# Moving the first 128 rows of w_down from the end of the load queue to its middle, as sixteen loads

## The chip, the cores and the metric

The kernel runs on one core of one Trainium2 chip. The metric is the device time of one execution in microseconds, as the median of several runs. A core has five engines with instruction streams of their own: TensorE (PE; its weight loads are listed as PEld), VectorE (DVE), ScalarE (ACT), GpSimd (POOL) and SyncE (SP). Here SP issues all but one of the loads from the chip's memory (HBM). A load is carried out by 16 DMA engines, each of which counts the load's semaphore up by one when its share has landed; whoever needs the data waits for the full count of 16.

## The reference

One token is decoded through an attention block and a gated MLP, with layer norms ahead and residual sums behind:

```python
scores = einsum("bhqd,bhkd->bhqk", q, k) * (Dh ** -0.5)   # q = layernorm(x) @ wq
p = softmax(scores);  o = einsum("bhqk,bhkd->bhqd", p, v)
h = x + o.reshape(B, Sq, Hq * Dh) @ wo
g = layernorm(h) @ w_gate;  u = layernorm(h) @ w_up
out = h + (gelu(g) * u) @ w_down
```

There are 32 heads of width 128, a cache of 4096 positions, a model width D of 640, and a hidden width DF of 1728. All inputs are bf16. K and V take 33.6 MB each; w_down, with 1728 x 640 elements, takes 2.2 MB.

## The kernel before

The heads are worked off in eight groups of four (`NG`, `HG`). For each group SP loads 4 MB of K and 4 MB of V. There are two buffers for each (`kbuf`, `vbuf`), so that the load of K for group n+2 waits until the last multiplication of group n has read its buffer (`kfree[n]`), and a V load until the products with V of two groups before are done (`vfree`). For each group DVE multiplies K by the query (L339), TensorE sums over the head width with an identity matrix (L348), DVE reduces (L355), ACT forms the exponentials (L384), and TensorE multiplies by V (L395). The work of neighbouring groups is interleaved by hand in the loop over n (from L453), and at the loop's end SP issues the next V and K loads; for n = 3 these are V of the fourth group and K of the sixth.

All order is written out by hand. The class `Sched` collects a list of instructions per engine with the semaphores that each waits for. What SP issues runs through one queue in the order of issue: wq, K 0, K 1, V 0, then K and V by turns, wo in two parts with the last V load between them, w_gate, w_up, and then w_down. The weights of the MLP lie over the K and V buffers (`over`), so w_gate, w_up and w_down wait for the last readers of these.

w_down is loaded in two ways. Its last 64 rows come in eight loads of four partitions (L581), which follow w_up in the queue. Its first 1664 rows are 13 column blocks of 128 rows; `WD_PARTS` groups these in loads of 5, 4, 3 and 1 blocks (L586). In a load of n blocks, partition p holds the n successive rows n*p to n*p+n-1 of the part; `WD_COLS` gives the columns of w_gate and w_up that belong to block s, so that the hidden values come out in the same order.

The tail runs like this. `up` multiplies the normed h by w_gate (into pg) and by w_up (into pu), 70 matmuls each (L648). DVE and ACT form gelu(g)*u, ending in `hm` (L664). Then for each of the 13 blocks and the two remainders four matmuls (L686) add to the output in PSUM. Their order is: five blocks; the small product `rest` (L670), which spreads the remainder's hidden values; four blocks; the two remainders; four blocks. Each waits for its own load. Then DVE copies the sum (L690), and SP writes it out (L691).

Of the kernel before, what the change touches and what calls it, by code (L numbers as in the profile page):

```python
# [6 lines left out]
BF16 = mybir.dt.bfloat16  # L7
# [4 lines left out]
D = 640  # L12
# [20 lines left out]
DJ = 128 // HW  # L33
NFT = 13
NF = NFT + 1
WD_PARTS = (5, 4, 3, 1)

WD_COLS = []
for _n in WD_PARTS:
    _b = 128 * len(WD_COLS)  # L40
# [73 lines left out]
def bass_sequential_preLN__gqa_block_cached__glu_gated_geglu__decode_kernel(  # L114
# [12 lines left out]
    S = Sched(nc)  # L127

    def sb(name, shape, dt):
        return nc.alloc_sbuf_tensor(name, shape, dt)  # L130
# [7 lines left out]
    def over(name, base, shape):  # L138
        return nc.alloc_sbuf_tensor_at(name, shape, BF16, offset=nc.lookup_mloc(base).addr)
# [3 lines left out]
    wg_sb = over("wg_sb", kbuf[NG % 2], [128, NC_D, DF])  # L143
    wu_sb = over("wu_sb", kbuf[(NG + 1) % 2], [128, NC_D, DF])
    wd_sb = over("wd_sb", vbuf[NG % 2], [128, NFT + NRR, D])

    NPR = 3
    prod = [sb("prod%d" % i, [128, RP, DH], BF16) for i in range(NPR)]
# [8 lines left out]
    xm = sb("xm", [VM, VR, DH], FP32)  # L157
# [7 lines left out]
    csel = sb("csel", [128, HW], BF16)  # L165
    jred = sb("jred", [128, DJ], FP32)
    cred = sb("cred", [128, HW], FP32)
    x_sb = sb("x_sb", [1, D], BF16)
    x32 = sb("x32", [128, NC_D], FP32)
    h32 = sb("h32", [128, NC_D], FP32)  # L170
    sq = sb("sq", [128, NC_D], FP32)
# [12 lines left out]
    hm = sb("hm", [128, NF], BF16)  # L184
# [65 lines left out]
    def cache(src, g):  # L250
        return src[0, g * HG:(g + 1) * HG, :, :].rearrange("h (q r) d -> (h q) r d", r=R)
# [4 lines left out]
    def load_k(g):  # L256
        d_k[g] = S.dma("sync", "k%d" % (g % 2), lambda s: s.dma_start(
            kbuf[g % 2][:, :, :], cache(A_k_cache, g)), [kfree[g - 2] if g >= 2 else None])


    def load_v(g):
        d_v[g] = []
        cuts = [0, R]
        for i in range(len(cuts) - 1):
            lo, hi = cuts[i], cuts[i + 1]
            tok = S.dma("sync", "v%d_%d" % (g % 2, i), lambda s, lo=lo, hi=hi: s.dma_start(
                vbuf[g % 2][:, lo:hi, :], cache(A_v_cache, g)[:, lo:hi, :]),
                [vfree[g - 2] if g >= 2 else None])
            d_v[g] += [tok] * (hi - lo)
# [44 lines left out]
    def query(g):  # L314
        tok = None
        for c in range(NC_D):
            n0 = g * HG * DH
            tok = S.op("tensor", lambda t, c=c, n0=n0: t.matmul(  # L318
                pq[:, :], xb[:, c, :], wq_sb[:, c, n0:n0 + HG * DH],
                start=(c == 0), stop=(c == NC_D - 1)),  # L320
                [t_xb, d_wq, t_qb[g - 1] if g else None], token=(c == NC_D - 1))
        for hh in range(HG):
            lo, hi = hh * PPH, (hh + 1) * PPH
            t_qb[g] = S.op("scalar", lambda a, lo=lo, hi=hi, hh=hh: a.copy(  # L324
                qb[lo:hi, g, :], pq[lo:hi, hh * DH:(hh + 1) * DH]), [tok])
        return tok
# [10 lines left out]
    def mult(g, s):  # L337
        n = g * NP + s
        return S.op("vector", lambda v: v.tensor_tensor(  # L339
            out=prod[n % NPR][:, :, :], in0=kbuf[g % 2][:, s * RP:(s + 1) * RP, :],  # L340
            in1=qb[:, g, :].unsqueeze(1).to_broadcast([128, RP, DH]), op=ALU.mult),
            [d_k[g], t_qb[g], fold_done.get(n - NPR)])

    def fold(g, s, t_mult):
        n = g * NP + s
        W = 512 // RP
        for j in range(DH // W):
            fold_done[n] = S.op("tensor", lambda t, j=j: t.matmul(  # L348
                pf[n % 2][:, :], Ibf[:, :], prod[n % NPR][:, :, j * W:(j + 1) * W],
                start=(j == 0), stop=(j == DH // W - 1)),  # L350
                [t_mult, t_ibf, red_done.get(n - 2)], token=(j == DH // W - 1))

    def red(g, s):
        n = g * NP + s
        red_done[n] = S.op("vector", lambda v: v.reduce_sum(  # L355
            sc[g % 2][:, s * RP:(s + 1) * RP],
            pf[n % 2][:, :].rearrange("p (r w) -> p r w", r=RP), axis=AX.X),
            [fold_done[n], t_exp[g - 2] if g >= 2 else None])
# [3 lines left out]
    def top(g):  # L362
        t_mx[g] = S.op("vector", lambda v: v.reduce_max(  # L363
            mx[:, g:g + 1], sc[g % 2][:, :], axis=AX.X), [red_done[g * NP + NP - 1]])

    def turn(g):
        t_mm[g] = S.op("tensor", lambda t: t.matmul(  # L367
            pm[0:1, 0:128], mx[:, g:g + 1], I32[:, :], start=True, stop=True),
            [t_mx[g], t_i32, t_exp[g - 1] if g else None])

    def head(g):
        t_mr[g] = S.op("vector", lambda v: v.reduce_max(  # L372
            mrow[0:1, g * HG:(g + 1) * HG],
            pm[0:1, 0:128].rearrange("p (h q) -> p h q", h=HG), axis=AX.X), [t_mm[g]])
# [46 lines left out]
    def total(w):  # L421
        t_zz[0] = S.op("tensor", lambda t: t.matmul(
            pz[:, 0:HW], ones[:, :], RS[:, w * HW:(w + 1) * HW], start=True, stop=True),
            [t_exp[2 * w + 1], t_aP[w - 1] if w else None])
# [14 lines left out]
    def place(w, b):  # L439
        t_aP[w] = S.op("vector", lambda v: v.tensor_copy(  # L440
            aP[:, w * HW:(w + 1) * HW], pz[:, 16:16 + HW]), [b])
# [4 lines left out]

    CH = NV // 4

    query(0)
    query(1)  # L450
    t_mul = {}
    t_g = None
    for n in range(NG - 1):  # L453
        w = (n - 3) // 2 if n >= 3 and n % 2 else None
        p, o = n - 1, n - 2
        beside = p >= 0 and n < NG - 2

        t_mul[0] = mult(n, 0)
        if p >= 0:
            red(p, NP - 1)  # L460
            top(p)
        if w is None and n >= 4:
            place((n - 4) // 2, t_g)
        t_mul[1] = mult(n, 1)

        fold(n, 0, t_mul[0])
        if p >= 0:
            turn(p)
            head(p)
        if o >= 0:  # L470
            values(o, 3 * CH, NV)
        fold(n, 1, t_mul[1])
        red(n, 0)
        t_mul[2] = mult(n, 2)
        if p >= 0:
            soft(p)
        if w is not None:
            total(w)
        if 2 <= n + 1 < NG:
            t_qlast = query(n + 1)  # L480
        fold(n, 2, t_mul[2])
        red(n, 1)
        if w is not None:
            invert(w)
        if o >= 0:
            extract(o)
        t_mul[3] = kfree[n] = mult(n, 3)
        if o >= 0:
            column(o)
        if beside:  # L490
            values(p, 0, CH)
        fold(n, 3, t_mul[3])
        red(n, 2)
        if w is not None:
            spread(w, [(po[:, w * HW:(w + 1) * HW], 0, HW, t_acc[o])])
        if beside:
            values(p, CH, 2 * CH)
        if w is not None:
            t_g = gather(w)
        if beside:  # L500
            values(p, 2 * CH, 3 * CH)

        if n == 0:
            load_k(2)
            load_v(1)
        elif n == NG - 3:
            load_k(n + 2)
            load_v(n)
        else:
            if n >= 2:  # L510
                load_v(n)
            if n + 2 < NG:
                load_k(n + 2)
# [65 lines left out]
    for h in range(2):  # L579
        for j in range(4):  # L580
            d_wdr = S.dma("sync", "wdr", lambda s, h=h, j=j: s.dma_start(  # L581
                wd_sb[32 * h + j:32 * h + NRP:4, NFT:NFT + NRR, :], rows[h, j]), [t_zr])
    d_wd = []
    for i, n in enumerate(WD_PARTS):
        s0 = len(d_wd)
        tok = S.dma("sync", "wd%d" % i, lambda s, s0=s0, n=n: s.dma_start(  # L586
            wd_sb[:, s0:s0 + n, :],
            B_w_down[128 * s0:128 * (s0 + n), :].rearrange("(p i) n -> p i n", i=n)), [vfree[NG - 2]])
        d_wd += [tok] * n
# [34 lines left out]
    NQ = D // 4  # L624
# [39 lines left out]
    t_hm = S.op("vector", lambda v: v.tensor_mul(hm[:, :], gu[:, :], pu[:, 0:NF * WIDE:WIDE]), [a, t_u])  # L664
# [9 lines left out]
    def down(s, j):  # L674
        if s >= NFT:
            return hr[0:NRK, s - NFT:s - NFT + 1], wd_sb[0:NRK, s, j * NQ:(j + 1) * NQ]
        return hm[:, s:s + 1], wd_sb[:, s, j * NQ:(j + 1) * NQ]

    n = sum(WD_PARTS[0:2])
    order = list(range(n)) + list(range(NFT, NFT + NRR)) + list(range(n, NFT))  # L680
    for i, s in enumerate(order):
        if s == WD_PARTS[0]:
            t_hr = rest()
        for j in range(4):
            last = i == len(order) - 1
            b = S.op("tensor", lambda t, s=s, j=j, last=last: t.matmul(  # L686
                pd[32 * j:32 * j + 1, 0:NQ], *down(s, j),
                start=False, stop=last, skip_group_check=True),
                [t_hr if s >= NFT else t_hm, d_wd[s]], token=(last and j == 3))
    t_o = S.op("vector", lambda v: v.tensor_copy(o_sb[:, :], pd[:, 0:NQ]), [b])  # L690
    d_o = S.dma("sync", "out", lambda s: s.dma_start(  # L691
        out[0, 0, :].rearrange("(j i) -> j i", j=4), o_sb[0:128:32, :]), [t_o])
# [32 lines left out]
```

## Time and profile before

| what | value |
|---|---|
| median of 3 runs | 203.91 us (203.9 to 204.17) |
| profiled execution: span from first to last instruction | 202.33 us |
| median less that span | 1.58 us |
| TensorE busy | 155.4 us, 77% of the span |
| VectorE busy | 116.4 us, 58% |
| ScalarE busy | 30.7 us, 15% |
| moved from HBM | 84.23 MB, 416 GB/s over the span |
| mean granted TensorE clock | 0.930 |

The page gives no other time for the profiled execution than its span, so sums are made against the span, and the 1.58 us between span and median stands for what lies around it. A line of the profile names an engine, a line of the kernel (L686), an operation, and output and input by name; "<-DMA wd_sb..." in brackets says what ended the idle time before it. PEld rows are weight loads of TensorE, which run ahead of the matmuls. "SPq" rows are issues of loads on SP. The DMA share of a stretch is the busy time of packets that start in it, over 16 engines. Below the views, the trace records each DMA packet with its start, duration and size, and each count of a load's semaphore; it does not record which of the 16 engines carried a packet.

### The profile page before, as it was taken

How to read it: one execution, taken by the hardware profiler on the slowest of the kernel's cores; microseconds unless marked ns; L12 is line 12 of the kernel's file. 1: busy time of each engine (PE TensorE's matmuls, PEld its weight loads, DVE VectorE, ACT ScalarE, POOL GpSimd, SP SyncE). 2: the span in 40 equal slices, each digit the busy share in tenths (PEclk: the TensorE clock that was granted, in tenths of full speed). 3: DMA queues.
4: the chain of work that ended last, by engine and by line, in shares of the span. 5: the costliest groups of instructions: out<-in, count | busy, mean ns of one | idle time of the engine just before them, and what ended most of it. 6: DMA issues, size and time to landing. Idle time of an engine off the chain costs nothing.

```text
span 202.3 us, 2515 instructions
## 1 busy us (share of the span) xinstructions
PE 155.4 (77%) x1084; PEld 71.0 (35%) x1084; DVE 116.4 (58%) x153; ACT 30.7 (15%) x110; POOL 2.4 (1%) x8
## 2 busy tenths in 40 slices
PE   1005349689959997996899499979777999978675
PEld 1001013233323432432343134324323344667562
DVE  6200087998097919953993488569999513301121
ACT  2002200007000600420060004200604004000000
POOL 1000000000000000000000000000000000200000
PEclk9999999999979999999999979999999999985555
DMA  7999999999999999999999999999999899999993
GB/s 259 437 437 415 421 441 473 428 415 415 418 453 460 421 416 415 424 449 447 428 428 415 424 447 447 421 434 415 428 444 441 380 429 461 441 383 437 434 388 117
DMA packets 3940, 84.38 MB, mean 417 GB/s; under 512 B 441, under 2 KB 570, under 8 KB 986
## 3 DMA queue, kind: packets, MB, share of 16 engines
q1 hardware_dynamic: 3928, 84.23, 97.4%
q8 instruction: 8, 0.13, 0.3%
q14 instruction: 2, 0.02, 0.0%
q10 hardware_dynamic: 2, 0.00, 0.0%
HBM read 84.23 MB, written 0.00 MB: 416 GB/s over the span
## 4 chain that ended last, share of the span: by engine, by line
DMA 59%; DVE 24%; PE 15%; issue 1%; SPq 0%; DVEq 0%
DMA kbuf<-in_A_k_cache_dram 46%; DVE prod L339 16%; DMA wu_sb<-in_B_w_up_dram 13%; PE pf L348 8%; PE pu L395 4%; DVE sc L355 3%; DVE xz L413 2%; PE pu L648 1%; DVE xm L410 1%; PE pf L686 1%; PE pg L395 1%; DVE mx L363 0%; DVE mrow L372 0%; PE pm L367 0%; SPq L247 0%
## 5 line engine op out<-in xcount | busy, mean ns | idle before, releaser
L339 DVE TENSOR_TENSOR prod<-kbuf,qb 128x4096 bf16<-128x4096 bf16 x32 | 72.8, 2278 | 45.0 <-DMA kbuf<-in_A_k_cache_dram 45.0
L348 PE MATMUL pf<-prod,Ibf 128*128 128x512 bf16 x256 | 66.5, 408 | 23.0 <-DVE prod L339 22.9
L348 PEld LDWEIGHTS pf<-prod,Ibf 128*128 128x128 bf16 x256 | 24.4, 103 | 62.3 <-DVE prod L339 29.5
L395 PE MATMUL pg<-vbuf,P 128*16 128x512 bf16 x128 | 29.9, 379 | 0.0
L355 DVE TENSOR_REDUCE sc<-pf 128x32 f32<-128x512 f32 x32 | 21.6, 676 | 4.8 <-PE pf L348 4.7
L395 PE MATMUL pu<-vbuf,P 128*16 128x512 bf16 x96 | 22.2, 379 | 0.0
L318 PE MATMUL pq<-wq_sb,xb 128*128 128x512 bf16 x40 | 12.1, 441 | 12.3 <-DMA wq_sb<-in_A_wq_dram 11.1
L380 ACT ACTIVATE nb<-pm 128x4 f32<-128x4 f32 x8 | 1.4, 175 | 118.5 <-PE pm L377 118.5
L384 ACT ACTIVATE P<-sc,nb 32x128 bf16<-32x128 f32 x32 | 18.6, 580 | 0.9
L395 PEld LDWEIGHTS pg<-vbuf,P 128*16 128x16 bf16 x128 | 10.6, 89 | 14.5 <-issue 1.3
L395 PEld LDWEIGHTS pu<-vbuf,P 128*16 128x16 bf16 x96 | 8.1, 90 | 11.7 <-issue 1.7
L324 ACT CAST qb<-pq 32x128 bf16<-32x128 f32 x32 | 8.2, 258 | 15.8 <-PE pq L318 15.0
L318 PEld LDWEIGHTS pq<-wq_sb,xb 128*128 128x128 bf16 x40 | 3.8, 110 | 17.1 <-issue 12.8
L384 ACT ACTIVATION_READ_ACCUMULATOR P<-sc,nb 32x1 f32 x32 | 8.0, 251 | 0.0
L601 PE MATMUL pf<-aP,wo_sb 128*128 128x32 bf16 x160 | 7.1, 194 | 0.8 <-issue 0.6
L413 DVE TENSOR_REDUCE xz<-xm 16x128 f32<-16x512 f32 x7 | 7.3, 1044 | 0.2
L601 PEld LDWEIGHTS pf<-aP,wo_sb 128*128 128x128 bf16 x160 | 6.8, 131 | 1.5 <-issue 1.1
L403 PE MATMUL pq<-P,vbuf 128*128 128x32 bf16 x128 | 3.6, 188 | 1.4 <-DMA vbuf<-in_A_v_cache_dram 1.4
L410 DVE TENSOR_TENSOR xm<-pg,rmask 16x512 f32<-16x512 f32 x4 | 2.7, 670 | 3.4 <-PE pg L395 3.4
L293 ACT ACTIVATE ln<-pz,ln 128x1 f32<-128x1 f32 x2 | 0.5, 263 | 23.9 <-DVE ln L290 23.9
L403 PEld LDWEIGHTS pq<-P,vbuf 128*128 128x128 bf16 x128 | 3.5, 104 | 1.5 <-DMA vbuf<-in_A_v_cache_dram 1.5
L410 DVE TENSOR_TENSOR xm<-pu,rmask 16x512 f32<-16x512 f32 x3 | 1.9, 643 | 3.2 <-PE pu L395 3.2
(84 smaller groups left out, 56.4 us busy)
## 6 DMA issues: line engine op xcount, KB each, us to landing
kbuf<-in_A_k_cache_dram SPq DMA_DIRECT2D x8, 4096.0 KB, 25.2
vbuf<-in_A_v_cache_dram SPq DMA_DIRECT2D x8, 4096.0 KB, 22.8
wq_sb<-in_A_wq_dram SPq DMA_DIRECT2D x1, 5120.0 KB, 15.1
wo_sb<-in_A_wo_dram SPq DMA_DIRECT2D x1, 3840.0 KB, 28.7
wg_sb<-in_B_w_gate_dram SPq DMA_DIRECT2D x1, 2160.0 KB, 22.5
wu_sb<-in_B_w_up_dram SPq DMA_DIRECT2D x1, 2160.0 KB, 27.1
wo_sb<-in_A_wo_dram SPq DMA_DIRECT2D x1, 1280.0 KB, 17.8
wd_sb<-in_B_w_down_dram SPq DMA_DIRECT2D x1, 800.0 KB, 15.8
```

The costliest lines, as they stand in the source:

```text
L318: tok = S.op("tensor", lambda t, c=c, n0=n0: t.matmul(pq[:, :], xb[:, c, :], wq_sb[:, c, n0:n0 + HG * DH], start=(c == 0), stop=(c == NC_D ...
L324: t_qb[g] = S.op("scalar", lambda a, lo=lo, hi=hi, hh=hh: a.copy(qb[lo:hi, g, :], pq[lo:hi, hh * DH:(hh + 1) * DH]), [tok])
L339: return S.op("vector", lambda v: v.tensor_tensor(out=prod[n % NPR][:, :, :], in0=kbuf[g % 2][:, s * RP:(s + 1) * RP, :], in1=qb[:, g, :]. ...
L348: fold_done[n] = S.op("tensor", lambda t, j=j: t.matmul(pf[n % 2][:, :], Ibf[:, :], prod[n % NPR][:, :, j * W:(j + 1) * W], start=(j == 0) ...
L355: red_done[n] = S.op("vector", lambda v: v.reduce_sum(sc[g % 2][:, s * RP:(s + 1) * RP], pf[n % 2][:, :].rearrange("p (r w) -> p r w", r=R ...
L384: t_exp[g] = S.op("scalar", lambda a, lo=lo, hi=hi, h=h, hh=hh: a.activation(P4[g % 2][lo:hi, :, hh], sc[g % 2][lo:hi, :], ACTF.Exp, bias= ...
L395: t_pv[g] = S.op("tensor", lambda t, i=i, r=r, last=last: t.matmul(pv[g % 2][0:VM, :], P4[g % 2][:, r:r + VR, :], vbuf[g % 2][:, r:r + VR, :],
L403: t_pv[g] = S.op("tensor", lambda t, r=r: t.matmul(pq[:, 0:WIDE], vbuf[g % 2][:, r, :], P4[g % 2][:, r, :].unsqueeze(1).to_broadcast([128, ...
L410: a = S.op("vector", lambda v: v.tensor_tensor(out=xm[:, :, :], in0=pv[g % 2][0:VM, :].rearrange("p (r d) -> p r d", r=VR), in1=rmask[:, : ...
L413: t_ext[g] = S.op("vector", lambda v: v.reduce_sum(xz[g % 2][:, :], xm[:, :, :].rearrange("p r d -> p d r"), axis=AX.X), [a, t_acc[g - 2] ...
L601: tok = S.op("tensor", lambda t, c=c, cc=cc, first=first, last=last: t.matmul(pp[:, cc * WIDE:(cc + 1) * WIDE], wo_sb[:, w, c, cc::NC_D], ...
L648: b = S.op("tensor", lambda t, s=s, c=c, part=part, first=first, last=last: t.matmul(ps[:, s * WIDE:(s + 1) * WIDE], part, hln[:, c:c + 1] ...
```

## The change

The first 128 rows of w_down get a tile of their own, `wd_pre`, and are loaded by sixteen loads of 15, 14, ..., 1 and 8 rows, issued by SP in the loop at n = 3, right after K of the sixth group. They have two semaphores, eight loads on each. The parts of w_down in the tail become 1, 5, 4, 2 and 1 blocks, of which the first is the moved one and is skipped there; the matmuls read block 0 from `wd_pre`, the small product comes after five blocks as before, and the remainders come after ten blocks instead of nine. To make room, `x_sb` lies over `xm`, which is written much later.

```diff
-WD_PARTS = (5, 4, 3, 1)
+WD_PARTS = (1, 5, 4, 2, 1)
+PRE = (15, 14, 13, 12, 11, 10, 9, 8, 7, 6, 5, 4, 3, 2, 1, 8)
...
+    wd_pre = sb("wd_pre", [128, D], BF16)
...
-    x_sb = sb("x_sb", [1, D], BF16)
+    x_sb = over("x_sb", xm, [1, D])
...
-        if n == 0:
+        if n == 3:
+            load_v(n)
+            load_k(n + 2)
+            p0 = 0
+            for m in PRE:
+                d_wpre = S.dma("sync", "wpre%d" % (len(d_pre) // 8), lambda s, p0=p0, m=m: s.dma_start(
+                    wd_pre[p0:p0 + m, :], B_w_down[p0:p0 + m, :]))
+                d_pre.append(d_wpre)
+                p0 += m
+        elif n == 0:
...
-    d_wd = []
+    d_wd = [d_pre[-1]]
     for i, n in enumerate(WD_PARTS):
+        if i == 0:
+            continue
         s0 = len(d_wd)
...
+        if s == 0:
+            return hm[:, 0:1], wd_pre[:, j * NQ:(j + 1) * NQ]
         return hm[:, s:s + 1], wd_sb[:, s, j * NQ:(j + 1) * NQ]
 
-    n = sum(WD_PARTS[0:2])
+    n = sum(WD_PARTS[0:3])
     order = list(range(n)) + list(range(NFT, NFT + NRR)) + list(range(n, NFT))
     for i, s in enumerate(order):
-        if s == WD_PARTS[0]:
+        if i == 5:
             t_hr = rest()
...
-                [t_hr if s >= NFT else t_hm, d_wd[s]], token=(last and j == 3))
+                [t_hr if s >= NFT else t_hm, d_wd[s], d_pre[7]], token=(last and j == 3))
```

More of the change, by code (lines that the diff above doesn't have):

```diff
@@ L447, in bass_sequential_preLN__gqa_block_cached__glu_gated_geglu__decode_kernel @@
     CH = NV // 4
+    d_pre = []
     query(0)
```

## The prediction

> **What bounds the kernel now.** I read the page first, for the share of each engine and of the DMA queues; then the chain of waits in its last 40 us; then the timeline of the weight loads and of SP's queue; then stretches of time for the DMA share; and last the trace's single DMA records: the 16 completion counts that every load sends, one from each DMA engine, and the times and sizes of packets. From the page:
>
> ```profile
> DMA  7999999999999999999999999999999899999993
> ...
> q1 hardware_dynamic: 3928, 84.23, 97.4%
> q8 instruction: 8, 0.13, 0.3%
> ```
>
> The one queue with all of SP's loads keeps the 16 DMA engines busy for 97.4% of the span. What comes later in it lands later, unless it lies in a gap. The second line counts eight fetches of instructions on the same engines; they matter below. From the chain of waits (start, us, what):
>
> ```profile
> 167.66 27.13 DMA wu_sb<-in_B_w_up_dram
> 194.79 0.05 issue
> 194.84 2.54 PE pu L648 x70
> 197.38 0.03 issue
> 197.41 0.02 DVEq L106
> 197.43 0.04 issue
> 197.47 0.18 DVE hm L664
> 197.65 0.04 issue
> 197.69 0.84 PE pf L686 x20
> ```
>
> The end hangs on the landing of w_up at 194.79; 2.90 us later the matmuls with w_down begin. The timeline of TensorE's weight loads shows a second tie:
>
> ```profile
> 198.57 0.36 PEld L686 LDWEIGHTS pf<-wd_sb,hm 128*1 128x1 bf16 x16
> 199.20 0.10 PEld L686 LDWEIGHTS pf<-wd_sb,hr 48*1 48x1 bf16 x8 [0.27 <-issue]
> 199.57 0.23 PEld L686 LDWEIGHTS pf<-wd_sb,hm 128*1 128x1 bf16 x12 [0.26 <-DMA wd_sb<-in_B_w_down_dram]
> 199.94 0.09 PEld L686 LDWEIGHTS pf<-wd_sb,hm 128*1 128x1 bf16 x4 [0.15 <-DMA wd_sb<-in_B_w_down_dram]
> ```
>
> The last two groups also wait for w_down, whose last load lands at 199.90. So two limits end within about 0.1 us of each other: TensorE's own pace after w_up, and the end of the queue. A gain needs both to come earlier; a loss needs only one of them later.
>
> The completion counts show that the 16 engines (I call them lanes) are not level. Those of w_up land at 192.98 to 193.20 (six lanes), 193.63, 193.90, 193.95, then 194.54 to 194.64 (five), 194.76 and 194.79. Each instruction fetch (16 KB, at 52.4, 85.0, 114.3, 150.5, 178.0, 185.4, 191.9 and 197.8) makes one further lane late by 1.6 to 1.8 us, for good. The eight loads of 4 partitions (L581) use four lanes, the same four each time: their 2560 B packets form four chains, one packet each 0.105 us, beginning at 192.53, 192.73, 193.18 and 193.49. So these four are none of the seven lanes late by a fetch, but two of them are late by 0.65 and 0.97. The chains add 0.84 us to these lanes alone; followed to the end, the third lands its last packet at 199.57 and the fourth at 199.90, which is the kernel's last landing.
>
> **The change part by part.** Sum against the profiled execution, span 202.33 us; the median of the runs, 203.91, lies 1.58 above it, and I add that at the end.
>
> *Issues on SP.* Timeline of SP:
>
> ```profile
> 88.05 0.33 SPq L257 DMA_DIRECT2D kbuf<-in_A_k_cache_dram  x1
> 100.78 0.33 SPq L266 DMA_DIRECT2D vbuf<-in_A_v_cache_dram  x1
> ...
> 175.80 5.10 SPq L581 DMA_DIRECT2D wd_sb<-in_B_w_down_dram  x8
> ```
>
> The sixteen issues follow K of the sixth group at 88.4. At 5.10/8 = 0.64 us each they take 10.2 us, to 98.6, while SP waits for the buffer of the next V load until 100.78. Cost nothing; the cover is SP's idle 12 us. If it were gone, that V load would be issued later, and it is only needed when the queue runs dry at about 112, a further 11 us. Unknown is whether 18 loads may be outstanding; the trace shows 15 (at 182.4, no stall of SP). No cost as the value, since 15 is near 18; its other end is among the rivals.
>
> *The moved rows, by lane.* The trace shows 128 partitions on 16 lanes, 4 on four, and the one-partition load of x as a single packet. By that a load of m rows puts one row on each of m lanes, the same first ones each time. Numbering lanes from 0, with the four of L581 as 0 to 3: lanes 0 to 7 get 16, 15, 14, 13, 12, 11, 10, 9 rows, lanes 8 to 14 get 7 down to 1, lane 15 none. A row is a 1280 B packet (the last load of before shows them 0.052 us apart) and a semaphore write of about 0.006: 0.058. Bounds: 0.052 for the bytes alone, 0.105 for a 2560 B load with its semaphore. I take 0.058. Lanes 0 to 3 carry 0.75 to 0.93 us more from 112 us on (upper bound 1.4 to 1.7), the mean lane 0.46, the last lane nothing.
>
> [...]
>
> *What leaves the tail.* The load of three column blocks becomes one of two: on every lane eight packets lose 1280 B, 8 x 0.05 = 0.40 us, after w_up. The loads of five, four and one blocks stay; the matmuls are the same 60, with 20 behind the small product (L670) where 16 were.
>
> *w_up.* All moved rows lie before it, so no lane brings it earlier. The seven late lanes are among 4 to 15, which of them no view tells. If they are the last seven, they get 0 to 6 rows: up to 0.35 more, from 194.54..194.79. If spread, the latest of them gets about ten rows, 0.58. The four known lanes: 193.95 + 0.75..0.93 = 194.70 to 194.88. w_up then lands 0.1 to 0.3 us later, or up to 0.6.
>
> *w_down, where I expect the stall.* The fourth chain's lane is already the last. Its share of the load of four blocks landed at 198.35; now 0.75 to 0.93 later, 199.10 to 199.28 (the tail loses its 0.40 only after that load). TensorE wants it after the first 24 matmuls and L670, at 198.57 + 0.10 = 198.67. The stall is 0.43 to 0.61, and what follows (L686's groups of 16, 8 and the rest, back to back) keeps its length, as both limits were tied. The last landing itself moves by 0.75..0.93 - 0.40 = +0.35 to +0.53, which says nearly the same.
>
> *Small things.* Two more waits ahead of the first w_down matmul, on loads that landed 80 us before: TensorE's semaphore instructions last 0.05, so 0 to 0.1. One more wait splits 4 matmuls from 16: at 199.94 such a wait followed a running group with no drain, so nothing; if it drained, 0.1 as between the groups at 198.57 and 199.20. x_sb over xm costs nothing: x is read at 2.1 us and xm first written after 46. The column order of w_gate and w_up changes strides only: 0.
>
> *Sum.* About +0.5 us by the w_down stall, in which w_up's 0.1 to 0.3 is contained: 202.33 + 0.50 + 1.58 = 204.4. Its own range: +0.35 to +0.65, 204.25 to 204.55.
>
> **The rivals.** *The late lanes are low-numbered.* Then w_up lands 0.4 to 0.6 later, and with the small waits the end moves by 0.6 to 1.0: 204.5 to 204.9. For it: twelve lanes, seven late, no view says which. Against: nothing but the count.
>
> *The first lanes are not late this time.* The two lags of 0.65 and 0.97 may come from short fetches: the records show two of 8 KB, at 74.0 and 88.5. If these fall on other lanes, lanes 0 to 3 end at 199.04 - 0.40 + 0.9 = 199.6, and only w_up's 0 to 0.3 is left: 203.9 to 204.2. Against: the three runs agree within 0.13%.
>
> *The rows travel in spare time* (faster). Stretches of the trace (us, then busy times, clock, DMA share, GB/s):
>
> ```profile
> 122.00:131.00 9.00, 9.00 (x43) 3.92 (x42) 6.58 (x9) 3.53 (x13) 0.00 (x0) 1.00 0.96 415
> 141.00:151.00 10.00, 7.75 (x37) 3.20 (x35) 9.93 (x10) 3.53 (x13) 0.00 (x0) 1.00 0.98 421
> ```
>
> Shares of 0.96 and 0.98 leave 0.4 and 0.2 us a lane. Were that true idle time, the mean 0.46 would fit in, w_up would land as before, the tail would be 0.40 lighter, and the two waits of 0.26 and 0.15 would go: up to -0.41, 203.5 to 203.8. It decides only if at least 0.46 us is spare on the late lanes. Against: the stretches beside them read 1.05, so the shares are packets counted at their start.
>
> *Fixed cost of sixteen small loads.* The eight small loads took 0.105 us each on a lane, so sixteen hold a lane under 1.7 us; this is inside the bounds. [...]
>
> *A queue limit, or another split.* If SP stalls at 16 outstanding loads, the V load after them is issued only when the sixth K has landed (113.9) and the lanes idle about 2 us: 206. If 15 or 13 rows go to one lane (the trace shows only 1, 4 and 16), lane 0 gets some 86 rows, 86 x 0.058 = 5 us: about 208.5.
>
> **How the numbers follow.** Forecast 0.50; low-numbered late lanes 0.17; first lanes not late 0.16; spare time 0.12; queue limit or split 0.05. 0.2% (0.41 us) is about what a measurement of this kernel can tell from no change. Of the forecast about a fifth lies under +0.41, so slower 0.40 + 0.17 + 0.05 = 0.62, same 0.10 + 0.16 = 0.26, faster 0.12. The predicted time is 204.4. The range takes in half of the spare-time case below and all of the low-numbered case above, but for its end with both small waits: 203.65 to 205.0.
>
> **What would show it.** Right: last completion count of w_up at 194.8 to 195.1; weight loads of L686 idle by 0.4 to 0.6 us on w_down ahead of the group of four blocks; last landing at 200.2 to 200.5; lanes 0 to 3 last; SP done with the sixteen issues before 100 and V loads issued as before. Wrong: w_down's last landing before 199.9 (the lanes were levelled), w_up earlier than 194.7, or a gap in the DMA row after 112 us.

## The result, and the profile after

The changed kernel takes 205.59 us (median of four runs, 205.49 to 205.72) against 203.91 for the kernel before. The ratio is 1.0084, with a 95% interval of 1.0069 to 1.0098: slower by 1.68 us, where I had forecast 204.4 and a range up to 205.0. The sign was right; the size was not.

The profiled execution took 205.62 us and has a span of 204.37. So what lies around a span is 1.25 us here. Sixteen other executions of the kernel before have a median of 203.77 us and spans of 202.4 to 202.6, which gives the same; the 1.58 that I added was 0.3 too much. By spans, then, the loss is 2.04 us between the two profiled executions, and about 1.85 between the usual ones (202.5 and 204.2 to 204.5).

The page of the changed kernel, its DMA row and its queues (packets, MB, share of 16 engines' span):

```profile
DMA  7999999999999999999999999999999999999991
...
q1 hardware_dynamic: 4184, 84.23, 97.1%
q8 instruction: 8, 0.13, 0.3%
```

The bytes are as before, and there are 256 packets more: 128 rows and 128 semaphore writes. The two semaphores took 92 and 36 counts, as many as their loads have rows: one row for each DMA engine that takes part in a load, as I had split them. No gap stands in the row; the queue is simply busy 2 us longer.

The chain of waits of the changed kernel (start, us, what):

```profile
169.04 27.79 DMA wu_sb<-in_B_w_up_dram
196.84 0.05 issue
196.88 2.52 PE pu L662 x70
199.40 0.03 issue
199.43 0.02 DVEq L107
199.45 0.04 issue
199.49 0.18 DVE hm L678
199.67 0.04 issue
199.72 0.84 PE pf L702 x20
200.55 0.12 PE pz L684
200.67 1.66 PE pf L702 x26
```

The last share of w_up landed at 196.84; before it was 194.79. From there to the end it is 7.53 us, against 7.54. So all of the loss is w_up's landing, and nothing behind it was gained or lost. The stall on w_down that I expected is missing, as the timeline of TensorE's weight loads shows:

```profile
200.48 0.10 PEld L684 LDWEIGHTS pz<-hq,hrow 128*128 128x128 bf16 x1 [0.27 <-issue]
200.60 0.49 PEld L702 LDWEIGHTS pf<-wd_sb,hm 128*1 128x1 bf16 x20
201.36 0.10 PEld L702 LDWEIGHTS pf<-wd_sb,hr 48*1 48x1 bf16 x8 [0.27 <-issue]
201.72 0.23 PEld L702 LDWEIGHTS pf<-wd_sb,hm 128*1 128x1 bf16 x12 [0.26 <-issue]
```

Where the kernel before had two idle times ended by a DMA of w_down, every idle time is now "issue". The last landing moved from 199.90 to 201.69, but w_up moved by more, so w_down was always there. The first of those two idle times has kept its 0.26 us although the load of w_down that this group begins with had landed at 201.29, 0.43 us ahead. So it was not the landing that made it in the kernel before either, and the tie that I had read in these lines was looser than I took it for.

SP's timeline shows that the issues themselves cost nothing:

```profile
89.67 0.33 SPq L259 DMA_DIRECT2D kbuf<-in_A_k_cache_dram  x1
90.03 5.70 SPq L511 DMA_DIRECT2D wd_pre<-in_B_w_down_dram  x16
100.95 0.36 SPq L268 DMA_DIRECT2D vbuf<-in_A_v_cache_dram  x1
```

Sixteen issues in 5.70 us, 0.36 each where I took 0.64, and the next V load is issued at 100.95 (before: 100.78).

So when did the queue fall behind? Every load of K, V and the weights over 128 partitions sends 16 completion counts. I took the mean time of the 16 for each load and subtracted the same mean of the kernel before:

```
load                       after less before, us
first loads of K                 +0.22
fourth V load                    +0.23
   (the sixteen small loads lie here, behind sixth K)
fifth V load                     +1.51
w_up                             +1.56
last loads of w_down             +1.17
```

0.22 us is there from the first load on, before anything differs in the queue; the other kernels below show -0.02 to +0.16 there, and I have no cause for it. Then, within the one stretch that holds the moved rows, 1.28 us come up, and they stay. The 0.40 that the tail should lose is there (1.56 to 1.17). From here on I use a measure that lies inside one execution: the mean of the fifth V load less that of the fourth. Before it is 19.53 us, after 20.82: **+1.29 us for 128 rows, 8 per engine on average, so 0.16 us a row.** I had 0.058, and 0.105 as the upper bound. The other half microsecond of w_up's +2.05 is its spread: its last count now comes 1.37 us behind its mean, before 0.89.

The stretches show the same (us, then busy times of PE, PEld, DVE, ACT and POOL, clock, DMA share, GB/s). Before:

```profile
110.00:113.00 3.00, 3.00 (x16) 1.19 (x14) 0.00 (x0) 0.00 (x0) 0.00 (x0) 1.00 1.09 470
113.00:116.00 3.00, 0.33 (x2) 0.00 (x0) 2.11 (x1) 0.00 (x0) 0.00 (x0) 0.97 0.94 399
```

After:

```profile
110.00:113.00 3.00, 3.00 (x15) 1.26 (x14) 0.00 (x0) 0.00 (x0) 0.00 (x0) 1.00 1.10 379
113.00:116.00 3.00, 0.49 (x3) 0.00 (x0) 1.39 (x1) 0.00 (x0) 0.00 (x0) 0.92 0.94 347
```

The DMA engines are as busy as before, but move less: 363 GB/s over the six microseconds instead of 435. The missing 72 GB/s x 6 us = 0.43 MB would take 1.0 us at 435 GB/s. The moved rows' own bytes are within the GB/s, so this is a loss on top of them. It can be seen in the packets too. A K or V packet of 32 KB normally takes 1.22 us. Of those that start between 110 and 118 us, 1 of 107 took over 1.3 us before; after, 35 of 86 did, up to 2.1 us. The excess over 1.22 adds up to 13 us, 0.8 us per DMA engine. So the big packets that travel beside the small rows became slow, and that is some two thirds of the 1.29; with the rows' own 0.46 it makes up nearly all of it.

### The profile page after: what moved, and what is told of

It reads as the page before. It is cut to its first block, busy times and chain, and to the rows that moved or that the text cites. A ratio compares the mean times of both kernels' runs of the same rounds, so it can differ in the third digit from the quotient of the medians.

```text
span 204.4 us, 2531 instructions
## 1 busy us (share of the span) xinstructions
PE 156.2 (76%) x1084; PEld 71.1 (35%) x1084; DVE 116.4 (57%) x153; ACT 30.6 (15%) x110; POOL 2.4 (1%) x8
## 4 chain that ended last, share of the span: by engine, by line
DMA 60%; DVE 28%; PE 10%; issue 1%; SPq 0%; DVEq 0%
DMA kbuf<-in_A_k_cache_dram 47%; DVE prod L341 19%; DMA wu_sb<-in_B_w_up_dram 14%; DVE sc L357 4%; PE pf L350 4%; PE pu L397 3%; DVE xz L415 2%; DVE xm L412 1%; PE pu L662 1%; PE pf L702 1%; DVE mx L365 1%; DVE mrow L374 0%; SPq L249 0%; DVE o_sb L706 0%; PE pm L369 0%
## 5 line engine op out<-in xcount | busy, mean ns | idle before, releaser
L397 PE MATMUL pu<-vbuf,P 128*16 128x512 bf16 x96 | 23.1, 390 | 0.0
L397 PEld LDWEIGHTS pg<-vbuf,P 128*16 128x16 bf16 x128 | 10.6, 89 | 14.5 <-issue 1.3
L662 PE MATMUL pu<-hln,wu_sb 128*128 128x32 bf16 x70 | 2.5, 194 | 1.7 <-DMA wu_sb<-in_B_w_up_dram 1.7
```

Source lines behind the costliest of these rows:

```text
L397: t_pv[g] = S.op("tensor", lambda t, i=i, r=r, last=last: t.matmul(pv[g % 2][0:VM, :], P4[g % 2][:, r:r + VR, :], vbuf[g % 2][:, r:r + VR, :],
L662: b = S.op("tensor", lambda t, s=s, c=c, part=part, first=first, last=last: t.matmul(ps[:, s * WIDE:(s + 1) * WIDE], part, hln[:, c:c + 1] ...
```

## The experiments

What makes the neighbours slow? All kernels are made from the changed one, and the local measure (fifth V load less fourth, 19.53 before) is read from one profiled execution each. Its scatter is small: a kernel with no rows there gave 19.52, and four kernels with eight loads of 16 rows there gave 20.61 to 20.71. Nothing else of SP's queue lies between the two loads but K of the sixth group and the moved rows; one 16 KB instruction fetch, at 113 to 115 us, is there in every kernel.

### Fewer rows on the first engines, and one load instead of many

`one`: a single load of 128 rows at the same place.

```diff
-PRE = (15, 14, 13, 12, 11, 10, 9, 8, 7, 6, 5, 4, 3, 2, 1, 8)
+PRE = (128,)
```

`eight`: eight equal loads of 16 rows. Both drop the second semaphore's wait (`d_pre[7]`), which is not needed there.

```diff
+PRE = (16,) * 8
```

> One load of 128 rows (16 DMA engines, 8 rows each) in place of the sixteen, at the same place of the queue; nothing else changed. Measure: the mean over the 16 completion counts of the fifth V load less that of the fourth, 19.53 us before and 20.82 us in the changed kernel, so +1.29 for the moved rows. Every theory expects about +0.42 here (8 rows x 0.052) and w_up some 0.45 later than before: 204.3 to 204.4 us. If the moved position alone were the cause of the loss, +1.29 and 205.6 us.

> Eight loads of 16 rows in place of the sixteen: every DMA engine gets 8 rows, so the engines' shares are level. Same measure (fifth V load less fourth, mean, over the 19.53 of before). Unequal shares (the prediction's theory): +0.46 and 204.4 us. Destination (many engines writing adjacent partitions at once hold each other up): +1.3 to 1.5 and 205.3 to 205.7 us. Source (adjacent rows read at once): the same. Small packets as such: +1.3.

`one` takes 204.14 us, ratio 1.0019 (1.0010 to 1.0028); the measure is 19.97, so the rows cost 0.44 us, their bytes and hardly more. `eight` takes 204.89, ratio 1.0066 (1.0041 to 1.0091); the measure is 20.67, so +1.14. With equal shares nearly all of this loss is still there: what I had built my sum on, that engines 0 to 3 get up to 16 rows and the last none, is not what makes it. But a mean of 16 counts cannot see how a loss is spread over the engines, and TensorE waits for the last count. `eight` and the five other kernels with equal shares (`eight_dst`, `eight_src`, `eight_spread`, `eight_sems`, `two`, below) take 1.12 to 1.35 us more than the kernel before beside them, the change 1.68; in their profiles w_up's last count comes at 196.14 to 196.37, in the change's at 196.84. The intervals of `eight` and the change overlap, but the six lie on one side: some 0.3 to 0.6 us of the loss seem to go with the unequal shares or the sixteen loads.

The chain of waits of `one`:

```profile
169.22 26.17 DMA wu_sb<-in_B_w_up_dram
195.39 0.05 issue
195.44 2.53 PE pu L662 x70
```

w_up at 195.39, 0.60 later than before, and the times are 0.37 us longer: this is what moving 128 rows ahead of w_up costs when the rows cost only their bytes.

### Neighbouring partitions, neighbouring rows in HBM

Each of the eight loads writes only 16 neighbouring partitions and reads 16 neighbouring rows, where the one covers all 128. `eight_dst` writes every eighth partition, `eight_src` reads every eighth row:

```diff
-                    wd_pre[p0:p0 + m, :], B_w_down[p0:p0 + m, :]))
+                    wd_pre[p0 // m:128:8, :], B_w_down[p0:p0 + m, :]))
```

```diff
+                    wd_pre[p0:p0 + m, :], B_w_down[p0 // m:128:8, :]))
```

> The eight loads of 16 rows, with each load's rows written 8 partitions apart (partitions j, j+8, ..., j+120) instead of to 16 adjacent ones; the rows are read as before. Block 0 is then multiplied with its rows in another order than its hidden values, so that part of the output is not the reference's; no work is left out. Destination theory: +0.4 to 0.8 and 204.3 to 204.8 us. Source theory and small packets as such: as the eight loads with adjacent partitions, +1.3.

> The eight loads of 16 rows, with each load's rows read 8 rows apart in memory (10 KB) and written to 16 adjacent partitions. Block 0's rows are in another order than its hidden values, so that part of the output is not the reference's; no work is left out. Source theory: +0.46 and 204.4 us. Destination theory and small packets as such: +1.3 to 1.5 and 205.3 to 205.7 us.

The measure is 20.71 and 20.61, the ratios 1.0065 (1.0050 to 1.0080) and 1.0059 (1.0042 to 1.0076): no different from `eight`. Neither spacing relieves anything.

### A crowd of small loads, one semaphore, the number of loads

`eight_spread` puts two of the eight loads behind each of four big ones (sixth, seventh and eighth K, sixth V); `eight_sems` gives each load a semaphore of its own (all eight are waited for ahead of the first matmul with w_down); `two` makes two loads of 64 rows.

```diff
+    def pre2():
+        for m in (16, 16):
...
-            p0 = 0
-            for m in PRE:
...
+            pre2()
```

```diff
-                d_wpre = S.dma("sync", "wpre%d" % (len(d_pre) // 8), lambda s, p0=p0, m=m: s.dma_start(
+                d_wpre = S.dma("sync", "wpre%d" % len(d_pre), lambda s, p0=p0, m=m: s.dma_start(
```

```diff
+PRE = (64,) * 2
```

> The eight loads of 16 rows, two each behind K of the sixth, seventh and eighth group and behind V of the sixth, instead of all eight behind K of the sixth. Measure: mean landing of w_up less mean landing of the fourth V load; before 91.09 us, eight loads together +1.16, one load +0.46. Theory A (a crowd: 128 completion counts from 16 engines within 3 us hold one another up): the crowd is gone, +0.46 to 0.6 and 204.1 to 204.4 us. Theory B (each engine pays for each small load, whenever it comes): +1.16 and 204.8 to 205.0 us.

> The eight loads of 16 rows together as before, but each with a semaphore of its own instead of one for all. If the counts queue up at the one semaphore: +0.46 to 0.6 in the same measure and 204.1 to 204.4 us. If what is held up is shared by all semaphores (theory A) or is paid per small load (theory B): +1.16 and 204.8 to 205.0 us.

> Two loads of 64 rows (4 rows on each of 16 engines) at the place of the eight. The rows of each engine are the same 8. Theory B, paid per load: the surplus of the eight loads over the one, 0.70, in proportion to the loads added, 0.70 x 1/7 = 0.10, so +0.56. Theory A, a crowd of 32 counts only: no surplus, +0.46. Both near 204.1 to 204.3 us; a surplus above 0.3 would mean that neither counts loads rightly.

All three stay slow: `eight_spread` 1.0061 (1.0046 to 1.0076), `eight_sems` 1.0057 (1.0042 to 1.0072), `two` 1.0062 (1.0046 to 1.0077). Spread over four places, the 32 rows behind sixth K cost 0.34 us (19.87), a little over a quarter of `eight`'s 1.14, and from the fourth V load to w_up all 128 rows cost 1.34 us (92.43 between the means, 91.09 before; in `eight` 92.25): the cost goes with the rows, wherever they are, and not with their crowding. The semaphore is not it (20.70). And two loads are as dear as eight (20.74), so neither the number of loads nor that of semaphore writes is it. What is left as the difference between `two` and `one` is that a load covers half of the partitions.

### The same row at the end of the queue

`one_tail` loads the 128 rows as one load right behind w_up and nothing in the loop.

```diff
-    d_wd = [d_pre[-1]]
+    d_wd = [S.dma("sync", "wpre0", lambda s: s.dma_start(wd_pre[:, :], B_w_down[0:128, :]))]
```

> The first 128 rows as one load again behind w_up, ahead of the load of five blocks; parts, tile and order of matmuls otherwise as in the changed kernel. If position alone makes the 0.37 us that one load in the middle lost: w_up as before (+0.0 in the same measure) and 203.7 to 203.9 us. If the new parts or the order of matmuls cost something themselves: 204.1 us or more with w_up as before.

```profile
167.69 27.16 DMA wu_sb<-in_B_w_up_dram
194.85 0.05 issue
194.90 2.52 PE pu L656 x70
```

203.84 us, ratio 1.0008 (0.9998 to 1.0017), and w_up at 194.85: the new grouping, the new tile, the place of the small product and `x_sb` over `xm` together cost nothing that these runs can tell. (The second semaphore's wait is not in it.) Against `one` this isolates the place in the queue: with the same single load, in the middle instead of behind w_up, w_up lands 195.39 instead of 194.85.

### Which partitions the rows go to

What remains is which partitions a small load writes. The eight loads of L581, each of four partitions 4 apart in the lower half, had left their neighbours alone: 15 of the 16 w_up packets beside them took 0.644 or 0.651 us, the usual time. Our trace does not name the engine of a packet, so these runs can show only whether the choice of partitions has an effect, not how it comes about.

Three kernels take eight loads of eight rows at the old place, and leave the other 64 rows to one load behind w_up. In `k8_own` a load writes eight partitions 4 apart in the lower half, in `k8_far` the same spacing in the upper half, in `k8_adj` eight neighbouring partitions of the lower half.

```diff
+            for q in range(8):
+                d_pre.append(S.dma("sync", "wpre0", lambda s, q=q: s.dma_start(
+                    wd_pre[32 * (q // 4) + q % 4:32 * (q // 4) + 32:4, :], B_w_down[32 * (q // 4) + q % 4:32 * (q // 4) + 32:4, :])))
...
+    d_half = S.dma("sync", "whalf", lambda s: s.dma_start(wd_pre[64:128, :], B_w_down[64:128, :]))
+    d_wd = [d_half]
```

```diff
+                    wd_pre[64 + 32 * (q // 4) + q % 4:64 + 32 * (q // 4) + 32:4, :], B_w_down[64 + 32 * (q // 4) + q % 4:64 + 32 * (q // 4) + 32:4, :])))
...
+    d_half = S.dma("sync", "whalf", lambda s: s.dma_start(wd_pre[0:64, :], B_w_down[0:64, :]))
```

```diff
+                    wd_pre[8 * q:8 * q + 8, :], B_w_down[8 * q:8 * q + 8, :])))
```

> [...] Here only 64 rows are moved to the middle, as eight loads of 8 rows, each to partitions 4 apart in the lower half (the spacing of the eight remainder loads, which showed no surplus); the other 64 rows come as one load behind w_up. Mean landing of w_up less that of the fourth V load: before 91.09 us, plus 64 x 0.058 / 16 = 0.23. [...] Any theory by which small or partial loads cost as such: surplus in proportion to rows, 0.70 x 64/128 = 0.35, so 91.65 to 91.7.

> [...] If partial loads cost as such: the same as with partitions 4 apart.

> [...] If it is adjacency within a load that costs: no surplus, 91.3 to 91.4.

The measure that I had named, w_up's mean less that of the fourth V load, comes to 92.48, 93.16 and 92.22 us, above every value expected, and is spoiled in all three. In `k8_own` the granted clock fell in a stretch where before it was at 1.00. The kernel before:

```profile
130.00:140.00 10.00, 8.94 (x42) 3.28 (x40) 6.62 (x8) 0.00 (x0) 0.00 (x0) 1.00 0.99 426
```

and `k8_own`:

```profile
130.00:140.00 10.00, 6.78 (x25) 2.15 (x23) 5.45 (x5) 0.00 (x0) 0.00 (x0) 0.76 1.02 439
```

```profile
169.42 0.34 SPq L267 DMA_DIRECT2D vbuf<-in_A_v_cache_dram  x1
```

TensorE did less there, its buffers came free later, and SP issued the last V load at 169.42 (in `k8_far` 167.19), when DMA engines had begun to run out of work (at 170.3 us only 9 of the 16 had a packet). `k8_adj` had the same at 0.78. In `k8_far` the loss is 0.88 us at the fifth V load and still 0.90 at w_gate; the last 0.24 come at w_up itself, whose last packets run beside the half load that I had put behind it: of its last 28, 22 took longer than 0.66 us, where 0.644 is usual.

The times (204.89, 205.41 and 205.58 us; ratios 1.0064 (1.0045 to 1.0084), 1.0096 (1.0066 to 1.0127) and 1.0091 (1.0074 to 1.0108)) are no clean test either, since in all three the other 64 rows lie right behind w_up as a load of half of the partitions. I fall back on the local measure, which ends before 140 us and was not named for these three beforehand: `k8_own` 19.92, `k8_adj` 20.28, `k8_far` 20.41. Less 0.23 us for four rows per engine on average at 0.058, the surplus is 0.16, 0.52 and 0.65. Of the K and V packets between 110 and 118 us, 13 of 100, 36 of 93 and 33 of 92 took over 1.3 us. The same eight loads of the same shape are thus four times as disturbing in the upper half as in the lower half. The rows' own packets agree: in `k8_own` each took 0.055 us, as in `one`, in `k8_far` 0.060 on average and up to 0.101. So it matters which partitions a small load writes; why it does, these runs do not show.

### The same size in two loads of all partitions

The cleanest test changes `two` so that both loads cover all 128 partitions, with half of the columns each: two loads and the same bytes, but 256 packets of 640 B.

```diff
-            p0 = 0
-            for m in PRE:
...
+            for c0 in (0, D // 2):
+                d_pre.append(S.dma("sync", "wpre0", lambda s, c0=c0: s.dma_start(
+                    wd_pre[:, c0:c0 + D // 2], B_w_down[0:128, c0:c0 + D // 2])))
```

> The first 128 rows in two loads at the same place, cut by columns: each load covers all 128 partitions with 320 of the 640 columns (640 B packets), where the two loads of before covered 64 partitions each. Number of loads, bytes, place and semaphore are the same. Measure: mean landing of the fifth V load less the fourth; before 19.53 us, two loads of 64 partitions 20.74, one load of 128 partitions 19.97. [...] If splitting as such costs: 20.7 and 204.9 to 205.0 us.

The stretches of `two`:

```profile
110.00:113.00 3.00, 3.00 (x16) 1.17 (x13) 0.00 (x0) 0.00 (x0) 0.00 (x0) 1.00 1.08 379
113.00:116.00 3.00, 0.25 (x2) 0.00 (x0) 1.38 (x1) 0.00 (x0) 0.00 (x0) 1.00 0.97 369
```

and of `two_cols`:

```profile
110.00:113.00 3.00, 3.00 (x15) 1.26 (x14) 0.00 (x0) 0.00 (x0) 0.00 (x0) 1.00 0.99 408
113.00:116.00 3.00, 0.45 (x3) 0.00 (x0) 1.95 (x1) 0.00 (x0) 0.00 (x0) 1.00 1.02 428
```

374 GB/s over the six microseconds against 418 (before: 435). The measure is 19.98, the same as `one`; 1 of 98 packets took over 1.3 us, in `two` 32 of 90. The time is 204.24 us, ratio 1.0011 (1.0000 to 1.0023), against 1.0062 for `two`. Twice as many small packets cost nothing more; covering all partitions takes the surplus away. The excess of the slow packets accounts for it: per DMA engine 0.74 us in `two` and 0.69 in `eight`, but 0.03 in `two_cols` and 0.07 in `one`.

In one table (the packets are those of K and V from 110 to 118 us that took over 1.3 us; the rows' cost is the measure less 19.53; each ratio is against runs of the kernel before taken beside it, whose median was 203.71 to 203.94 us):

| kernel | moved rows there | us | ratio | rows' cost, us | slow packets |
|---|---|---|---|---|---|
| before | none | 203.91 | | | 1 of 107 |
| `one_tail` | none | 203.84 | 1.0008 | -0.01 | 1 of 108 |
| `one` | 1 x 128 partitions | 204.14 | 1.0019 | 0.44 | 1 of 96 |
| `two_cols` | 2 x 128, half the columns | 204.24 | 1.0011 | 0.45 | 1 of 98 |
| `two` | 2 x 64 | 204.96 | 1.0062 | 1.21 | 32 of 90 |
| `eight` | 8 x 16 | 204.89 | 1.0066 | 1.14 | 38 of 89 |
| the change | 15, 14, ... 1, 8 | 205.59 | 1.0084 | 1.29 | 35 of 86 |

No version was faster than the kernel before.

## Why the prediction was right or wrong

*Issues on SP: right.* They were hidden as said, at 0.36 us each instead of 0.64; 18 loads in flight stopped nothing, so the queue limit falls.

*The moved rows, by lane: here the forecast failed.* The split was as I had it (256 packets more). The term "a row = 0.058 us, at most 0.105" was wrong: it measured 0.16 on average. The row's own bytes do cost what I took (8 x 0.058 = 0.46; `one` 0.44, `two_cols` 0.45). What was missing is the other part, 0.85 us, and it does not stand in the rows' own packets, which take only 67 ns, but in the K and V packets that run beside them. I priced a packet by its own duration and forgot to ask whom it delays. My upper bound came from the loads of L581. They write partitions 4 apart in the lower half, as `k8_own` does, which had the least surplus of the three (0.16 us). The trace of the kernel before shows that they do no harm: of the 16 w_up packets that start beside them, from 192.5 us on, 15 took 0.644 or 0.651 us, the usual time. So the row that I took as nearest was of another kind than the moved ones.

*The unequal shares: there as forecast, but not where most of the loss comes from.* In the mean, eight equal loads cost 1.14 and the change 1.29. The first lanes can be followed by their chains of 2560 B packets: w_up's count comes 0.45 us after a chain's first packet (before: 192.53 and 192.98). In the change w_up's counts on these four lanes moved by 2.08 us on average and the other twelve by 1.38, a difference of 0.70 where my rows give 0.50 (14.5 rows against 5.8 at 0.058, in one execution); in the six kernels with equal shares the two differ by 0.09 at most. But the two last counts of w_up, 196.43 and 196.84, are on other lanes.

*What leaves the tail: right in size* (0.38 against 0.40), *but of no use.* The tail of the queue is not what ends the kernel any more.

*w_up: the direction was right, the size was not.* I said 0.1 to 0.3, or up to 0.6 us later; it was 2.05 later in the profiled executions: 0.22 from the start of the execution, 1.29 at the moved rows, 0.05 behind them, and 0.48 in a wider spread of its counts. Had the rows cost their bytes alone, 0.6 would have been right: `one` has 194.79 to 195.39.

*w_down, where I expected the stall: wrong.* I had two tied limits and thought the second would move by more. Both moved together: w_up by 2.05, the load of four blocks, at which I saw the stall, by 2.15 (198.35 to 200.50), which is within the 0.2 us that it had to spare (it was wanted at 198.57), and the last landing by 1.79, since the tail's saving helps only what lies behind that load. So w_up alone sets the end, 7.53 us after it.

*Small things: right, zero.* `one_tail`, which has all of them but the second semaphore's wait, is within the measurement of the kernel before; with that wait, in the change, 7.54 became 7.53.

*The rivals.* "The late lanes are low-numbered" gave 204.5 to 204.9 and a w_up 0.4 to 0.6 later; it is nearest in its outcome, but not in its cause. "The first lanes are not late this time" gave 203.9 to 204.2, below what was measured. "The rows travel in spare time" falls with `one`: even the cheapest form of the rows moves the end by 0.37 us. The queue has no spare time, so whatever is put ahead of w_up brings w_up later by its bytes at least.

What stays open: the 0.22 us at the start of the changed kernel's profile; how the unequal shares reach w_up's last count, if they do. (That count's distance from the mean was 1.10 us at the fifth V load and 0.97 at wo's first part, less than before, 1.26 and 1.16; it grew to 1.46 at w_gate, before 0.98, with instruction fetches at 179.8 and 187.1 us in between, and the trace does not name the engines that these held up.) Open are also why the surplus depends on which partitions a load writes (0.16 us in `k8_own`, 0.65 in `k8_far`), and its size: `two` costs as much as `eight` (1.21 and 1.14 us).

## What to carry to other kernels

In a queue that never runs dry, moving a load forward gains nothing by itself: it delays all that it is moved ahead of by its bytes (in `one`, w_up came 0.60 us later and the end 0.37), so look first at which load the end hangs on. If a small piece must go in between, load it over all 128 partitions, with fewer columns rather than fewer partitions: here the same 164 KB cost 0.45 us that way and 1.14 to 1.29 us as loads of 16 or fewer rows. A packet's price is not only its own duration (0.067 us here, where a row cost 0.16); compare the durations of the packets beside it, in a trace of loads that cover the same partitions. A load that only looks alike can mislead: those of L581 left their neighbours alone (15 of 16 packets at their usual time).

## What the runs showed of the hardware

That a 1280 B packet (0.055 us in `one`, 0.067 on average in the change) can slow 32 KB packets beside it from 1.22 to as much as 2.1 us, with all engines still shown as busy (share 1.10 and 0.94, at 363 GB/s in place of 435), I had not expected; nor that loads of 64 partitions do this as much as loads of 16 (1.21 and 1.14 us), and loads of 128 not at all. Halving the packets to 640 B cost nothing (19.98 us against 19.97). And SP issues loads of few rows in 0.25 to 0.48 us each, sixteen of them one after the other without a stall.
